# Linear attention and a gated mixture of experts on one core: a list scheduler writes the order, v is copied beside ones, and the first token is routed first

## Chip, cores and metric

One core of one Trainium2 chip runs the whole program. The metric is the device time of one execution in microseconds (us), lower is better. A difference of about 1% is what a measurement of this kernel can tell from no change.

## What is computed

Eight batches (B = 8) of 576 tokens, eight heads of 64 columns. First linear attention for each head, then a mixture of experts whose input x is the attention's output with all heads side by side (512 columns).

```
phi(x) = where(x > 0, x, exp(x) - 1) + 1          # elu + 1
kv = phi(k).T @ v ;  z = sum over s of phi(k)      # 64 x 64 and 64, per head
x  = (phi(q) @ kv) / (phi(q) . z + 1e-6)
logits = x @ w_gate            # 8 experts
local  = sigmoid(x @ w_local)
for s in tokens:
    e = argmax(logits[s]) if s == 0 or local[s] < 0.5 else the expert of token s-1
    p = softmax(logits[s])
    out[s] = p[e] * (relu(x[s] @ w1[e]) @ w2[e])   # w1 512 x 1024, w2 1024 x 512
```

The kernel computes each batch with the expert of its first token and counts on the way the tokens for which another one would be due (`bad`). Only if that count is above 0 does a general path (`general`) run behind it.

## The kernel before

**Tiles.** The eight heads of a batch are two groups `j` of four, so there are 16 pieces `n = 2*a + j` of q, k and v (576 KB each in f32). A piece lies as 128 partitions x 2 x 9 x 64: a partition holds nine consecutive tokens (`c` = 0..8) of a head, 64 partitions a head.

**Attention of a piece.** `exps` (ScalarE, L158) makes exp of k or q; `phi` (VectorE) makes elu + 1 in one of two forms. With `both` ScalarE also does a Relu (L160) and VectorE one operation (L165); without it VectorE does two (L169, L170). `kvs` (TensorE, L179) accumulates the k-v product over the nine `c` in f32, four 64 x 64 tiles of the array at a time. Its moving operand is 128 columns wide: 64 of v and, by a strided view (`vones`), 64 ones that stand once behind each v slot; one column of the sums is z, the other 63 are not read. `kv` is copied out by VectorE (L184). `q_main` and `q_last` transpose q in f32 (L192), ScalarE copies the result out (L203, L212). `num_main` and `num_last` make numerator and denominator (L235, L250, 65 columns), `divide` (VectorE, L218 to L221) divides into bf16 `xb`, `x_part` and `x_last` transpose that (L262, L270) and VectorE copies it into `xT_all` (L264, L271).

**Router.** `logits` (L282, L288) and its copy (L290). The first token of a batch stands in chunk 0, one of the four large chunks, so `pick` (L296 to L310) comes behind the large chunks of a batch. It finds the expert on VectorE, loads the index into a GpSimd register, and GpSimd issues the loads of that expert's w1 and w2 (4 MB in HBM, cast to bf16 on the way). `spread` makes the gate of each token on VectorE.

**Experts.** `hidden(b, m)`, m = 0..7: eight products of 128 x 288 (L364) and a Relu on ScalarE (L367). `output(b, i)`, i = 0..4: L381 for four chunks and L390 for the small one, scaled and copied by ScalarE (L383, L394), which also issues the stores (L386, L396).

**Order.** All engines run in order, in the order in which the program calls these functions, and that is written by hand: batches 0 and 1's attention first, then for each batch `b` the 13 steps (`hidden` 8, `output` 5), and behind each step `s` a piece of the attention of batch b+2 (`after(b, s)`). Each function holds its matrix work and the copy out of PSUM behind it, so an engine's work stands in the order of the steps. The loads of k, q and v go through SyncE's queue; a slot's next load is issued behind the work that frees it (`load_k` in `kvs`, and so on). k and q have three slots each, v four.

## Time and profile before

| | us |
|---|---|
| time, median of 3 runs | 321.84 (320.71 to 323.48) |
| the profiled execution, time | 319.24 |
| its span on the core | 317.5 |
| TensorE busy in the span | 245.4 (77%) |
| VectorE busy | 143.6 (45%) |
| ScalarE busy | 133.2 (42%) |
| GpSimd busy | 16.1 (5%) |
| stretch to the first `hidden` | 67.7 |
| a stage with attention beside the experts (172.02 to 206.46) | 34.44 |
| a stage of the experts alone (275.77 to 293.40) | 17.63 |

A stage here runs from the first `hidden` of a batch to the first `hidden` of the next one. TensorE's clock has two levels, 1.2 and 2.4 GHz; the profile gives the granted clock of a stretch as a share of 2.4 GHz. The profile's busy time of TensorE is that of its matmuls; the weight loads overlap them and are listed apart (PEld). An idle time in brackets behind a row is that of the engine just before the row, with what ended it.

### The profile page before, as it was taken

What the parts mean: (1) busy time and instruction counts of PE and PEld (TensorE: products, weight loads), DVE (VectorE), ACT (ScalarE), POOL (GpSimd) and SP (SyncE); (2) the same over time, 40 slices, a digit from 0 to 9 for tenths busy, and PEclk for the clock granted to TensorE, in tenths of its full rate; (3) what the DMA queues carried; (4) which work ended last, traced back from release to release, by engine and by line L of the source; (5) the groups of instructions that cost most, each with busy time, mean ns of one, the idle gap of its engine ahead of it and who ended that gap; (6) DMA issues with size and microseconds to landing.
All of it is one profiled execution on the core that took longest, in us unless ns stands there. A gap on an engine that the chain in (4) does not pass through costs nothing.

```text
span 317.5 us, 10444 instructions
## 1 busy us (share of the span) xinstructions
PE 245.4 (77%) x4706; PEld 177.0 (56%) x4706; DVE 143.6 (45%) x406; ACT 133.2 (42%) x202; POOL 16.1 (5%) x27
## 2 busy tenths in 40 slices
PE   0635767479779869986998878986798699999891
PEld 0625756357645657464765665564656476675640
DVE  0324373756624565448454762375444844330000
ACT  4545422333137434453346414642455323363541
POOL 1000300001000200001000200020001000020000
PEclk9976578758999999999999999999999979999997
DMA  7991799408980599439973799069513960297304
GB/s 227 391 391 39 198 261 258 152 0 166 257 296 3 163 256 286 163 150 181 267 271 132 147 265 322 4 181 240 85 67 150 166 104 4 97 192 126 151 2 154
DMA packets 29809, 55.27 MB, mean 174 GB/s; under 512 B 2624, under 2 KB 12864, under 8 KB 28736
## 3 DMA queue, kind: packets, MB, share of 16 engines
q0 software_dynamic: 13088, 16.78, 32.0%
q1 hardware_dynamic: 13056, 28.31, 25.1%
q10 hardware_dynamic: 3616, 9.46, 7.9%
q8 instruction: 39, 0.64, 0.8%
q14 instruction: 10, 0.08, 0.1%
HBM read 61.88 MB, written 9.44 MB: 225 GB/s over the span
## 4 chain that ended last, share of the span: by engine, by line
PE 63%; DVE 18%; issue 9%; DMA 3%; ACT 3%; ACTq 2%; SPq 1%; DVEq 0%
PE yps L381 18%; PE hps L364 15%; PE kvps L179 13%; PE nps L235 6%; PE tq L192 4%; DMA qraw<-in_q_dram 3%; PE tx L262 3%; DVE kraw L170 3%; DVE qraw L170 3%; DVE qraw L169 2%; PE yps L390 2%; DVE kraw L169 1%; PE tql L192 1%; PE lps L288 1%; ACTq L386 1%
## 5 line engine op out<-in xcount | busy, mean ns | idle before, releaser
L364 PE MATMUL hps<-xT_all,w1b 128*128 128x288 bf16 x512 | 73.7, 291 | 4.2 <-issue 2.2
L367 ACT ACTIVATE hT<-hps 128x576 bf16<-128x576 f32 x64 | 41.3, 649 | 80.7 <-PE hps L364 74.3
L179 PE MATMUL kvps<-vraw,kraw 64*64 64x128 f32 x1152 | 43.4, 310 | 35.5 <-DVE kraw L170 15.2
L179 PEld LDWEIGHTS kvps<-vraw,kraw 64*64 64x64 f32 x1152 | 39.1, 157 | 40.0 <-DVE kraw L170 17.0
L381 PE MATMUL yps<-w2b,hT 128*128 128x512 bf16 x256 | 59.8, 379 | 0.6 <-issue 0.6
L364 PEld LDWEIGHTS <-w1b 128*128 128x128 bf16 x512 | 46.6, 99 | 19.7 <-issue 7.1
L381 PEld LDWEIGHTS <-hT 128*128 128x128 bf16 x256 | 23.5, 98 | 25.8 <-issue 0.9
L383 ACT ACTIVATE yo<-yps,pr 128x512 f32<-128x512 f32 x32 | 22.0, 688 | 37.4 <-PE yps L381 37.4
L192 PE MATMUL tq<-ident,qraw 64*64 64x64 f32 x1024 | 21.2, 236 | 12.7 <-issue 8.7
L203 ACT COPY qT<-tq 128x512 f32<-128x512 f32 x32 | 18.0, 617 | 30.4 <-PE tq L192 29.7
L192 PEld LDWEIGHTS tq<-ident,qraw 64*64 64x64 f32 x1024 | 18.9, 148 | 16.6 <-issue 12.8
L235 PE MATMUL nps<-kv,qT 64*64 64x65 f32 x1024 | 23.7, 232 | 2.8 <-issue 1.9
L235 PEld LDWEIGHTS nps<-kv,qT 64*64 64x64 f32 x1024 | 19.8, 144 | 8.9 <-issue 7.5
L218 DVE TENSOR_SCALAR den<-nps 128x8 f32<-128x8 f32 x32 | 5.3, 165 | 42.0 <-PE nps L235 41.8
L184 DVE COPY kv<-kvps 128x130 f32<-128x130 f32 x16 | 4.7, 294 | 42.1 <-PE kvps L179 42.1
L221 DVE TENSOR_TENSOR xb<-nps,rec 128x512 bf16<-128x512 f32 x32 | 22.1, 691 | 1.1
L158 ACT ACTIVATE ex<-qraw 128x1152 f32<-128x1152 f32 x16 | 18.5, 1158 | 7.2 <-DVE lt_all L290 6.5
L305 POOL DMA_DIRECT2D w1b<-in_moe_w_dram x9 | 6.9, 766 | 262.7 <-DVE e0f L300 166.0
L158 ACT ACTIVATE ex<-kraw 128x1152 f32<-128x1152 f32 x16 | 18.5, 1156 | 3.6 <-DMA kraw<-in_k_dram 3.6
L264 DVE COPY xT_all<-tx 128x1024 bf16<-128x1024 bf16 (+1 forms) x20 | 11.6, 580 | 11.7 <-PE tx L262 11.7
L170 DVE TENSOR_TENSOR kraw<-kraw,ex 128x1152 f32<-128x1152 f32 x12 | 16.3, 1359 | 0.4
L170 DVE TENSOR_TENSOR qraw<-qraw,ex 128x1152 f32<-128x1152 f32 x12 | 16.3, 1359 | 0.4
(71 smaller groups left out, 178.6 us busy)
## 6 DMA issues: line engine op xcount, KB each, us to landing
kraw<-in_k_dram SPq DMA_DIRECT2D x16, 576.0 KB, 8.5
vraw<-in_v_dram SPq DMA_DIRECT2D x16, 576.0 KB, 10.1
qraw<-in_q_dram SPq DMA_DIRECT2D x16, 576.0 KB, 5.9
out_dram<-yo ACTq DMA_DIRECT2D x16, 512.0 KB, 3.7
w1b<-in_moe_w_dram POOLq DMA_DIRECT2D x7, 1024.0 KB, 10.0
w2b<-in_moe_w_dram POOLq DMA_DIRECT2D x7, 1024.0 KB, 18.3
w1b<-in_moe_w_dram POOLq DMA_DIRECT2D x2, 512.0 KB, 9.0
w2b<-in_moe_w_dram POOLq DMA_DIRECT2D x2, 512.0 KB, 15.1
```

What stands on the lines that cost most here:

```text
L158: nc.scalar.activation(ex_[n, x], raw_, Act.Exp)
L170: nc.vector.tensor_tensor(r, r, e, op=Alu.min)
L179: nc.tensor.matmul(ps[g * PH:(g + 1) * PH, t, :2 * Dh], lhsT=f[t * PH:(t + 1) * PH, g, c, :], rhs=vones(t, s, g, c), start=(c == 0), stop= ...
L192: nc.tensor.matmul(ps[g * PH:(g + 1) * PH, t, at * PH:(at + 1) * PH], lhsT=slot(n, "q")[h, g, c, :], rhs=ident[h, h], start=True, stop=True)
L203: nc.scalar.copy(qT[n][:, t, :SM].rearrange("q (i p r) -> q r i p", i=NC - 1, r=2), ps[:, t, :].rearrange("q (r i p) -> q r i p", i=NC - 1 ...
L221: nc.vector.tensor_tensor(dst, ps[:, :, :, :Dh], rec.rearrange("p g (m o) -> p g m o", o=1).to_broadcast([P, 2, m, Dh]), op=Alu.mult)
L235: nc.tensor.matmul(ps[o * PH:(o + 1) * PH, g, (il * 2 + t) * W:(il * 2 + t + 1) * W], lhsT=qT[n][g * PH:(g + 1) * PH, t, i * P + o * PH:i ...
L264: nc.vector.tensor_copy(xT[a][:, 2 * j:2 * j + 2, i0 * P:i1 * P], ps[:, j, :2 * n].rearrange("p (g s) -> p g s", g=2))
L364: nc.tensor.matmul(ps[:, u, :HS], lhsT=w1b[:, kk, m * P:(m + 1) * P], rhs=xT[b][:, kk, u * HS:(u + 1) * HS], start=(kk == 0), stop=(kk == ...
L367: nc.scalar.activation(hT[b][:, m, :].rearrange("p (u s) -> p u s", u=2), ps[:, :, :HS], Act.Relu)
L381: nc.tensor.matmul(ps[:, 0, :], lhsT=hT[b][:, m, i * P:(i + 1) * P], rhs=w2b[:, m, :], start=(m == 0), stop=(m == FK - 1))
L383: nc.scalar.activation(ym[:, i, :], ps[:, 0, :], Act.Copy, scale=pr[:, i:i + 1])
```

## The change

**Order.** Each function is split into its matrix part and the part that empties PSUM (`kvs` and `kv_out`, and so on). A list of operations with an engine, a length, a rank, needs and a PSUM slot is built in the program, and `in_order` runs a greedy schedule over it; the functions are called in the order that comes out. The stages still lie two batches behind the attention (LEAD = 2) by rank, but the first `hidden` of batch 0 no longer stands behind batch 1's attention.

**v beside ones.** A v piece is copied into `vone` (two buffers, 65 columns for each `c`, the last one all ones), by GpSimd for 15 of 16 pieces and by ScalarE for piece 1. The moving operand of the k-v product is 65 columns wide.

**First token.** The nine token columns are dealt out anew: `c` = 0, with the first token, is the small chunk. q's `c` = 0 of batch 0 is loaded, activated and transposed by itself, first of all. `logits` is done in two parts, the small chunk first, and `pick` follows the small one. w1 and w2 are each issued as one load, also for batch 0, which had two halves.

**phi.** k takes the `both` form in all pieces but piece 0; q as before (`both` in batches 0 and 1 alone). The large chunks' transposes are done for both groups in one PSUM tile with one copy. v has three slots instead of four, the exp buffers are three instead of four.

The core of the diff:

```diff
-        NV = 4
+        NV = 3
+        NE = 3
+        vone = [raw.tile([P, 2, C, W], F32, name=f"vone{i}") for i in range(2)]
...
         def load_q(n):
-            if n < B * NJ:
+            if n < NJ:
+                load(qraw[n % NR][:, :, 1:, :].rearrange("p g c d -> p g (c d)"), q, n, 1, C)
+            elif n < B * NJ:
                 load(qraw[n % NR].rearrange("p g c d -> p g (c d)"), q, n)
+
+        def load_q0(n):
+            load(qraw[n % NR][:, :, 0, :], q, n, 0, 1)
...
+        def v_ones(n):
+            if n == 1:
+                nc.scalar.copy(vone[n % 2][:, :, :, :Dh], vraw[n % NV])
+            else:
+                nc.gpsimd.tensor_copy(vone[n % 2][:, :, :, :Dh], vraw[n % NV])
+
         def kvs(n):
...
-                        nc.tensor.matmul(
-                            ps[g * PH:(g + 1) * PH, t, :2 * Dh],
-                            lhsT=f[t * PH:(t + 1) * PH, g, c, :],
-                            rhs=vones(t, s, g, c), start=(c == 0), stop=(c == C - 1))
+                        nc.tensor.matmul(ps[g * PH:(g + 1) * PH, t, :W], lhsT=f[h, g, c, :],
+                                         rhs=vo[h, g, c, :], start=(c == 0), stop=(c == C - 1))
+
+        def kv_out(n):
             kv[n] = kvp.tile([P, 2, W], F32, name="kv")
-            nc.vector.tensor_copy(kv[n], ps[:, :, :W])
-            load_k(n + NR)
-            load_v(n + NV)
+            nc.vector.tensor_copy(kv[n], open_.pop(("K", n))[:, :, :W])
...
-            nc.vector.max_with_indices(m8, i8, lt_all[0:1, b, 0, :E])
+            nc.vector.max_with_indices(m8, i8, lt_all[0:1, b, NC - 1, :E])
...
+                op(("VC", n), "ACT" if n == 1 else "POOL", 1.16 if n == 1 else 1.8, r - 10, [("lat", "v", n), n >= 2 and ("K", n - 2)],
+                   lambda n=n: v_ones(n))
+                op(("K", n), "PE", 1.25, r, [("P", "k", n), ("VC", n)], lambda n=n: kvs(n), takes="a")
...
+            op(("PK", a), "DVE", 0.45, at - 3, [("RC", a, 0)], lambda a=a: pick(a))
+            for x in range(2):
+                op(("W", a, x), "POOL", 1.0, at + x,
+                   [("PK", a), a >= NW and (("H", a - NW, FK - 1) if x == 0 else ("O", a - NW, NC - 1)),
+                    x and ("W", a, 0)], lambda a=a, x=x: weights(a, x))
...
+                op(("H", a, m), "PE", 1.0, a * NU + m,
+                   [("WL", a, 0), ("XC", a, 0), ("XC", a, 1), ("XLC", a), ("H", a, m - 1) if m else a and ("O", a - 1, NC - 1)],
+                   lambda a=a, m=m: hidden(a, m), takes="m")
...
+        order, begun, done = in_order(ops, {"a": 2, "m": 2, "e": NE}, 0.2)
 
         with tc.manual_schedule():
-
-            for j in range(NJ):
-                exps(j, "k", True)
-                phi(j, "k", True)
-                kvs(j)
...
+            for name in order:
+                run[name]()
```

What `in_order` does at each engine that is free:

```diff
+            for op in queue:
+                name, _, length, rank, needs, takes, gives = op
+                at = now
+                for d in needs:
+                    if d not in done:
+                        break
+                    at = max(at, done[d] + (0.0 if of[d][1] == e else hop))
+                else:
+                    if takes:
+                        if not left[takes]:
+                            continue
+                        at = max(at, left[takes][0])
+                    if at > now:
+                        nxt.append(at)
+                        soon.append((rank, at))
+                    elif best is None or rank < best[3]:
+                        best = op
+            if best and any(r < best[3] - near and t < now + patience * best[2] for r, t in soon):
+                best = None
```

**What stands where now.** TensorE at the start of the program, before (kvps is the k-v product, tq the large q transposes, nps the numerators):

```order
L179 MATMUL kvps<-vraw_77,kraw_71 64x128 x36
L179 MATMUL kvps<-vraw_78,kraw_72 64x128 x36
L192 MATMUL tq<-ident,qraw_74 64x64 x32
L192 MATMUL tq<-ident,qraw_75 64x64 x32
L235 MATMUL nps<-kv,qT 64x65 x32
L262 LDWEIGHTS xb
L262 MATMUL tx<-identb,xb 128x128
```

and of the change (tql and npl belong to the small chunk, lps are its logits):

```order
L252 MATMUL tql<-ident,qraw_74 64x64 x4
L252 MATMUL tql<-ident,qraw_75 64x64 x4
L241 MATMUL kvps<-vone_80,kraw_71 64x65 x36
L241 MATMUL kvps<-vone_81,kraw_72 64x65 x36
L318 MATMUL npl<-kv,qT 64x65 x8
L345 LDWEIGHTS xb_272
L345 MATMUL txl<-identb,xb_272 128x128
...
L252 MATMUL tq<-ident,qraw_74 64x64 x32
L359 LDWEIGHTS xT_all
L359 MATMUL lps<-wg,xT_all 64x9
```

The small chunk's numerators, transposes and logits now stand ahead of the large chunks' numerators; one f32 matmul of this list is two in the profile, so x36 here is x72 there.

VectorE at the boundary of two stages, before (L290 is the copy of the logits, L169 and L170 are phi, L184 the copy of kv):

```order
L290 COPY lt_all<-lps 128x45
L169 TENSOR_SCALAR kraw_71<-kraw_71 128x1152
L170 TENSOR_TENSOR kraw_71<-kraw_71,ex 128x1152
L296 MAX m_2980<-lt_all 1x8
L296 MAX_INDEX i_2981<-m_2980,lt_all 1x8
L300 CAST e0f<-i_2981 1x1
L184 COPY kv<-kvps 128x130
L169 TENSOR_SCALAR qraw_74<-qraw_74 128x1152
L170 TENSOR_TENSOR qraw_74<-qraw_74,ex 128x1152
```

and of the change (L221, L223 and L224 are phi, L338 and L370 the copies of the large chunks' x and logits, L412 the first operation of the gates):

```order
L287 TENSOR_TENSOR xb_2354<-nps,rec_2425 128x512
L221 SCALAR_TENSOR_TENSOR kraw_71<-ex,kraw_71 128x1152
L338 COPY xT_all<-tx 128x4x256 x2
L223 TENSOR_SCALAR qraw_74<-qraw_74 128x1152
L224 TENSOR_TENSOR qraw_74<-qraw_74,ex 128x1152
L370 COPY lt_all<-lps 128x36
L412 TENSOR_REDUCE mx<-lt_all 128x5
```

All four phi of the next stage's pieces (the other two stand some rows further up) are now done ahead of the large chunks' logits, where before phi of k stood behind them and the second k's phi behind the gates.

GpSimd in the middle of the program, before:

```order
L297 TENSOR_LOAD i_1931
L305 ISA
L305 DMA w1b<-in_moe_w_dram 128x4x1024
L310 ISA
L310 DMA w2b<-in_moe_w_dram 128x8x512
```

and of the change (L232 are the copies of v):

```order
L232 COPY vone_80<-vraw_79 128x18x64
L232 COPY vone_81<-vraw_77 128x18x64
L385 TENSOR_LOAD i_1822
L388 ISA
L388 DMA w1b<-in_moe_w_dram 128x4x1024
L392 ISA
L392 DMA w2b<-in_moe_w_dram 128x8x512
```

Two copies now stand between a batch's weight loads and the next one's.

## Rows read from the trace of the kernel before

**Rows 1.** The page: span, and busy time of each engine.

```profile
span 317.5 us, 10444 instructions
PE 245.4 (77%) x4706; PEld 177.0 (56%) x4706; DVE 143.6 (45%) x406; ACT 133.2 (42%) x202; POOL 16.1 (5%) x27
```

**Rows 2.** Busy time by stage: window, us, each engine's busy, granted clock, DMA share, GB/s.

```profile
0.00:67.70 67.70, 35.25 (x951) 31.44 (x952) 28.64 (x82) 29.27 (x35) 4.28 (x13) 0.77 0.75 225
67.70:104.52 36.82, 31.54 (x591) 22.34 (x589) 18.28 (x50) 13.65 (x22) 1.62 (x2) 0.92 0.62 156
...
172.02:206.46 34.44, 28.85 (x591) 20.34 (x589) 18.56 (x50) 15.21 (x24) 1.64 (x2) 1.00 0.75 201
...
275.77:293.40 17.63, 16.97 (x126) 10.89 (x123) 3.70 (x22) 8.45 (x14) 1.63 (x2) 1.00 0.91 187
293.40:317.50 24.10, 15.68 (x110) 9.62 (x108) 0.30 (x2) 8.80 (x14) 0.00 (x0) 0.90 0.26 101
```

**Rows 3.** Timeline, TensorE in the stage from 172.02: start, us, instructions, idle before.

```profile
174.42 2.20 PE L179 MATMUL kvps<-vraw,kraw 64*64 64x128 f32 x72 [1.40 <-issue]
...
179.40 1.16 PE L192 MATMUL tq<-ident,qraw 64*64 64x64 f32 x64 [0.31 <-PE hps L364]
...
184.19 2.20 PE L179 MATMUL kvps<-vraw,kraw 64*64 64x128 f32 x72 [2.54 <-DVE kraw L170]
...
194.91 0.69 PE L235 MATMUL nps<-kv,qT 64*64 64x65 f32 x30 [1.35 <-issue]
```

**Rows 4.** Timeline of the same stage: phi on VectorE, and GpSimd.

```profile
172.18 0.75 DVE L169 TENSOR_SCALAR kraw<-kraw 128x1152 f32<-128x1152 f32 x1
...
176.43 0.89 POOL L310 DMA_DIRECT2D w2b<-in_moe_w_dram  x1
176.88 1.02 DVE L169 TENSOR_SCALAR qraw<-qraw 128x1152 f32<-128x1152 f32 x1
182.77 1.36 DVE L170 TENSOR_TENSOR kraw<-kraw,ex 128x1152 f32<-128x1152 f32 x1
```

**Rows 5.** Chain that ended last, pieces of the same stage: start, us, what.

```profile
187.47 0.63 PE nps L235 x32
...
189.18 1.09 PE tq L192 x64
```

**Rows 6.** Timeline of the start: first loads, products at the lower clock, first pick.

```profile
8.90 1.16 ACT L158 ACTIVATE ex<-kraw 128x1152 f32<-128x1152 f32 x1 [1.26 <-DMA kraw<-in_k_dram]
25.23 1.99 PE L192 MATMUL tq<-ident,qraw 64*64 64x64 f32 x64 [4.89 <-issue]
26.96 1.12 PE L235 MATMUL nps<-kv,qT 64*64 64x65 f32 x32
33.08 0.14 DVE L300 CAST e0f<-i 1x1 f32<-1x1 uint32 x1
34.35 1.63 POOL L305 DMA_DIRECT2D w1b<-in_moe_w_dram  x2 [32.49 <-issue]
```

**Rows 7.** Groups by line and shape: busy, mean ns of one, idle before.

```profile
L165 DVE SCALAR_TENSOR_TENSOR kraw<-ex,kraw 128x1152 f32<-128x1152 f32 x4 | 5.4, 1353 | 6.2 <-ACT kraw L160 6.2
L160 ACT ACTIVATE kraw<-kraw 128x1152 f32<-128x1152 f32 x4 | 4.7, 1163 | 0.1
L221 DVE TENSOR_TENSOR xb<-nps,rec 128x512 bf16<-128x512 f32 x32 | 22.1, 691 | 1.1
L264 DVE COPY xT_all<-tx 128x1024 bf16<-128x1024 bf16 x12 | 8.2, 685 | 8.5 <-PE tx L262 8.5
L126 POOL CAST identb<-ident 128x128 bf16<-128x128 f32 x1 | 0.3, 288 | 0.0
L130 POOL CAST iof<-ioi 128x8 f32<-128x8 int32 x1 | 0.2, 187 | 0.0
```

**Rows 8.** DMA issues: what, queue, count, KB each, median us to landing.

```profile
w1b<-in_moe_w_dram POOLq DMA_DIRECT2D x7, 1024.0 KB, 10.0
w2b<-in_moe_w_dram POOLq DMA_DIRECT2D x7, 1024.0 KB, 18.3
```

More of the change, by code (lines that the diff above doesn't have):

```diff
@@ new lines, in output_out, with op, qslots @@
+                    nc.scalar.dma_start(out=o[:, 0, h * (D // 2):(h + 1) * (D // 2)],
+                                        in_=yl[h * PH:(h + 1) * PH])
+        ops, run = [], {}
+        def op(name, eng, length, rank, needs, fn, takes=None, gives=None):
+            ops.append((name, eng, length, rank, [d for d in needs if d], takes, gives))
+            run[name] = fn
+        NU = FK + NC
+        def qslots(a):
+            old = [n - NQ for n in (a * NJ, a * NJ + 1) if n >= NQ]
+            return [("N", n // NJ, n % NJ, h) for n in old for h in range(2)] +                    [("NL", n // NJ) for n in old]
```

463 lines of the change are left out of this document (247 added, 216 removed).

## The prediction

> **What bounds the kernel now.** I read the page's busy line first, then busy time by stage, then the timeline of one stage, the chain that ended last, and the start. The busy line shows TensorE at 245.4 of 317.5 us and no other engine above half [rows 1], but that is a mean over parts with different limits. By stage [rows 2] there are three:
>
> - the start, 67.70 us in which TensorE has only 35.25 of work, at a mean granted clock of 0.77, and no `hidden` runs;
> - six stages with attention beside the experts, from 67.70 to 275.77, so 34.7 each; the one read closely is 34.44 long with 28.85 of TensorE work at full clock;
> - two stages of experts alone, 17.63 and 24.10 (the last with the final stores), nearly full of work.
>
> So 5.6 us of a middle stage are waits, and the timeline names them [rows 3]: 1.40 and 2.54 ahead of the two k-v products, 0.31 ahead of the q transposes, 1.35 within the numerators; they sum to 5.60. The 2.54 end with phi of k on VectorE (182.77 + 1.36 = 184.13, the product starts at 184.19) [rows 3, 4]. The 1.40 carries the label "issue", but phi of the first k began at 172.18 and takes 0.75 + 1.36 [rows 4], so it ended at 174.3 where the product starts at 174.42 [rows 3]: the same wait. The 1.35 has no releaser; I count it as staying.
>
> **The change, part by part.** All terms are for the profiled execution: 317.5 span, time 319.24, so 1.7 lie outside the span. The median of the runs is 321.84, 2.6 above that execution.
>
> *k-v product, 65 columns for 128.* One piece has 72 matmuls in 2.20, 31 ns each [rows 3]. No 65-column product that accumulates is in the trace. Nearest rows on the same four tiles with as many weight loads: 32 numerators of 65 columns in 0.63, 20 ns each, and 64 transposes of 64 columns in 1.09, 17 ns each [rows 5]. So a piece comes to 1.23 to 1.42 and saves 0.78 to 0.97; I take 0.87, 1.75 per stage. TensorE's work is the largest of a middle stage, so it counts in full: 28.85 - 1.75 = 27.1 of work per stage.
>
> *v copied on GpSimd.* Two copies of 1152 columns per stage. The only copies of that engine in the trace are 128 columns in 288 ns and 8 columns in 187 ns [rows 7]: 0.84 ns for each further column gives 1.15 us, all of 288/128 per column gives 2.6; I take 2. GpSimd has 1.64 of work in 34.44 [rows 2], and a copy can start when the product two pieces back is done, about a stage ahead, so it costs nothing but at the very start. It frees the v slot at the copy instead of at the product, which pays for the fourth slot. Behind the copies on GpSimd's queue stand the weight loads of a batch two stages away, and behind a w2 load, which waits for the last `output` of its buffer, stand copies wanted a stage later: no one is waiting for either.
>
> *phi of k with Relu on ScalarE.* VectorE: 1.35 instead of 0.75 + 1.36 for k [rows 4, 7], 1.5 less per stage, 18.56 to 17.1. ScalarE: two Relu of 1.16 more [rows 7], 15.21 to 17.5; its four store issues, not counted as busy, add some 2.5. Both stay far under 27.1, so nothing from this alone.
>
> *Order.* The order shows phi of both k of a stage ahead of the large logits of the stage before, so the 1.40 and 2.54 go; what is late next is ScalarE at a boundary (last `output` copy, four store issues, then the Relu of the new `hidden`), and there a k-v product and q transposes now stand between the `hidden`s as cover. I keep the 1.35 and allow 0.5 for the rest: 27.1 + 1.9 = 29.0 per stage. Bounds: 27.1 (no wait) and 32.7 (5.6 of waits as now).
>
> *The start.* By the order, the first `hidden` stands behind batch 0's attention and one k-v product, not behind two batches. Worked along its path: the second k was in ScalarE's hands at 8.90, when three large loads had landed [rows 6]; with two small ones ahead the first v is there at about 9.5. Copy 2 (11.5). Two k-v products at the lower clock: 32 numerators took 1.12 there [rows 6], so 72 take 2.5 each (16.5). Then the small chunk to the pick. Before went from its numerators at 26.96 to the pick's end at 33.22 [rows 6], 6.3 for the same kinds of step; the new path is shorter by half its numerators but has 64 transposes of 1.99 in front of the logits [rows 6]: 6 (22.5). From pick to weight issue 33.22 to 34.35, 1.1 [rows 6], and w1 lands 10.0 later [rows 8]: 33.6. Beside that VectorE has, behind the pick, four phi (5.4), four divisions (0.69 and two small operations, about 1.2 each: 4.8) and two copies of 0.7 [rows 7]: 11.6, to 34.1, then a k-v product and logits at the lower clock. First `hidden` at **36**; 33 if phases fall well, 44 if w1 takes the 18.3 that w2's median is [rows 8].
>
> *The first stage* then carries two batches of attention. Experts alone are 16.97 with some small work [rows 2], say 16.4, so attention is 28.85 - 16.4 = 12.4 before and 10.7 now. 16.4 + 2 x 10.7 - 1.4 (the product done early) = 36.4. The stage that now comes first has 31.54 of work against 28.85, 2.7 for the clock that is still low at its beginning (0.92) [rows 2]; with 2 x 1.9 of waits: 43.
>
> *Sum.* 36 + 43 + 5 x 29.0 + 17.63 + 24.10 = 265.7 span, 267.4 with the 1.7 outside, against 319.24. Between that and the same saving off the median (270) I give 268.
>
> **A rule against it.** In the row at 176.88 a one-input operation of VectorE took 1.02 instead of 0.75 while GpSimd was issuing a load [rows 4], so the two hinder one another, and copies of v are far longer users. The Trainium skill (GPSIMD Engine Reference, section 8, Key points) says that GpSimd shares its SBUF interfaces with VectorE and collides with operations in a two-port mode or with two SBUF inputs, and calls VectorE the better place for elementwise work. The row agrees with the first of these. As a mechanism of this kernel: if a copy of length c shuts VectorE out for its whole length, VectorE needs 17.1 + 2c per stage. With c = 2 that is 21.1, under 27.1, and costs nothing; it rules from c = 5.9 (28.9).
>
> **Rivals.**
>
> *Waits come back in the new order (B).* The order was fixed beforehand with lengths; where an engine is late, everything behind it waits. For it: PSUM for attention has two tiles; DMA is busy 0.75 of 34.44 [rows 2], 25.8, which is 89% of a stage of 29.0, so loads may come late. Against: each load is wanted most of a stage after it can be issued. 5 per stage: 36 + 46 + 5 x 32.1 + 41.7 + 1.7 = 286.
>
> *The start does not shorten so far (C).* If routing, copy and weights string out and the first `hidden` begins at 55: 19 more, 287. For it: ScalarE has 13 activations of q and k in a row before its first large q copies are out. Against: before reached its first pick at 33 with a whole large chunk in front.
>
> *GpSimd rules (D), the other side.* The place is VectorE's phi, shut out by copies. The stage at which nothing is gained: 317.5 = 36 + (s + 14) + 5s + 41.7, s = 37.6, so c = 10.3; at c = 11, s = 39.1 and the time is 328. For it: no f32 copy of that length is in the trace. Against: 288 ns for 128 columns is a fifth of the price per column that this needs. Short of it, c = 8 gives 33.1 per stage, about 292.
>
> *No waits at all (E).* 33 + 39 + 5 x 27.1 + 41.7 + 1.7 = 251.
>
> **How the numbers follow.** My forecast, own range 256 to 280: 0.62. B 0.17, C 0.08, D 0.06 (half of it short of the break-even point, half within 1% or slower), E 0.07. Leaving out D, the lower half of E and the upper third of B and C (0.18 together) gives 252 to 289. Only D's half ends at no gain (0.01 within 1%) or slower by over 1% (0.02; with 0.01 for what I have not thought of 0.03), so faster by over 1% is 0.96; 1% is about what a measurement of this kernel can tell.
>
> **What would show it.** Right: first `hidden` near 36; 72 k-v matmuls in 1.2 to 1.4; middle stages of 29 with at most 2 of idle TensorE; no k-v product that waits for phi. GpSimd copies near 2 with VectorE's phi at most a few tenths longer. Wrong: TensorE idle ahead of the numerators or `hidden` for ScalarE's copies (B), w1 landing after 40 or the pick after 30 (C), copies above 6 or phi far above 1.36 (D).

## The result and the profile after

| | before | after |
|---|---|---|
| time, median of 4 runs each, same chip | 322.66 us (320.71 to 324.56) | 280.22 us (278.88 to 282.19) |
| ratio, 95% interval | | 0.869 (0.861 to 0.877) |
| the profiled execution: time, span | 319.24, 317.5 | 279.97, 278.2 |
| stretch to the first `hidden` | 67.6 | 35.9 |
| the first stage | 36.8 | 43.5 |
| the next five stages together | 171.4 | 156.1 |
| the two stages of experts alone | 41.7 | 42.75 |

The kernel is 13% faster, and of the 39.3 us that the profiled span lost, 25.0 lie in the start and the first stage together, 15.3 in the next five stages; 1.0 is given back at the end. The kernel before is cut here at its first `hidden` itself, 67.56; the 67.70 of the earlier table lies 0.14 behind it. Here and below, medians are over all executions of a kernel, while ratios leave out its slower ones, so where the two disagree the ratio decides. The page of the changed kernel, which answers to [rows 1]:

```profile
span 278.2 us, 10449 instructions
PE 225.1 (81%) x4689; PEld 161.5 (58%) x4706; DVE 140.3 (50%) x396; ACT 146.8 (53%) x218; POOL 35.1 (13%) x42
...
q8 instruction: 39, 0.64, 0.9%
```

TensorE works 20.3 us less and idles 19.0 less. Busy time by stage, cut at the first `hidden` of each batch (as [rows 2]: window, us, busy of PE, PEld, DVE, ACT, POOL, granted clock, DMA share, GB/s):

```profile
0.00:35.87 35.87, 19.27 (x549) 16.97 (x550) 21.22 (x40) 25.97 (x31) 8.99 (x17) 0.76 0.97 300
35.87:79.38 43.51, 35.47 (x896) 25.73 (x897) 29.82 (x84) 23.60 (x36) 6.02 (x6) 0.92 0.90 247
79.38:115.64 36.26, 30.34 (x689) 22.45 (x688) 24.08 (x66) 20.83 (x30) 5.42 (x6) 0.95 0.89 222
115.64:146.05 30.41, 26.43 (x593) 18.86 (x591) 19.26 (x53) 16.94 (x26) 3.94 (x4) 1.00 0.90 224
146.05:177.34 31.29, 28.15 (x587) 19.50 (x589) 17.88 (x50) 17.39 (x26) 3.93 (x4) 0.95 0.82 202
177.34:206.98 29.64, 26.51 (x587) 18.85 (x588) 14.43 (x47) 13.91 (x23) 4.30 (x4) 1.00 0.69 153
206.98:235.45 28.47, 26.60 (x588) 18.91 (x589) 10.81 (x43) 10.78 (x20) 1.64 (x2) 1.00 0.61 118
```

From 35.87 to 235.45, 199.58 us, TensorE has 173.5 of work and 26.1 of idle time. The timeline of TensorE shows what is idle there (start, us, instructions, idle before; two stretches of the stage from 115.64, as [rows 3]):

```profile
117.69 1.28 PE L241 MATMUL kvps<-vone,kraw 64*64 64x65 f32 x72
...
123.83 1.16 PE L241 MATMUL kvps<-vone,kraw 64*64 64x65 f32 x63
126.72 0.35 PE L241 MATMUL kvps<-vone,kraw 64*64 64x65 f32 x9 [1.73 <-issue]
126.89 0.65 PE L299 MATMUL nps<-kv,qT 64*64 64x65 f32 x32
...
130.04 1.04 PE L252 MATMUL tq<-ident,qraw 64*64 64x64 f32 x55
132.88 0.38 PE L252 MATMUL tq<-ident,qraw 64*64 64x64 f32 x9 [1.81 <-issue]
```

From the first `hidden` on, no k-v product waits for phi in front of it any more, as [rows 3] had it twice per stage. Instead a product stops in its middle, nine matmuls before its end, and TensorE stays idle though the profile shows no engine that it waits for. Such an idle time is called a hole below. There are eleven between 35.87 and 235.45, from 1.14 to 3.59 us, 22.3 us together, and all the rest of the idle time is 3.8. The DMA view holds what they have in common. The queue named instruction moves packets of 0.64 MB / 39 = 16 KB; two of its rows (number of packets, MB, share of 16 engines), the first from the window 124.4 to 124.5, the second from 130.45 to 130.5:

```profile
q8 instruction: 1, 0.02, 57.6%
q8 instruction: 1, 0.02, 122.1%
```

57.6% of 16 engines in 0.1 us is 0.92 us of one engine, 122.1% in 0.05 us is 0.98. So one packet ends at 125.4 and TensorE goes on at 126.72, the other at 131.45 and it goes on at 132.88. All eleven holes end 1.2 to 1.5 us after the end of such a packet. Counted in TensorE's records (weight loads and matmuls), they stand on one grid: 126.72 and 132.88 are 257 apart, and every distance from one hole to the next is 1, 3, 4 or 5 times 256, within 3. The packets that end a hole take 0.9 to 1.1 us, no longer than others (0.9 to 1.5), so what is late is their start. The theory that follows, FETCH: TensorE had used up the instructions that it had, and the next ones came late.

Where four of the holes end (at 46.24, 69.62, 101.31 and 155.10; they are 1.82 to 3.59 long) the granted clock is also low: 0.50, the level of 1.2 GHz, from 46.1 to 49.5, 70.1 to 73.4, 100.9 to 104.1 and 155.5 to 158.7. Everywhere else between 35.87 and 235.45 it is at the upper level. So a hole seems to cost more than its idle time; that it is the reason for the lower clock was not tested by itself.

The start (as [rows 6]), first copy of v, pick, weight issue and first `hidden`, and three groups (as [rows 5, 7]: busy, mean ns of one, idle before):

```profile
9.57 1.31 POOL L232 COPY vone<-vraw 128x1152 f32<-128x1152 f32 x1 [7.62 <-DMA vraw<-in_v_dram]
...
20.63 0.14 DVE L378 CAST e0f<-i 1x1 f32<-1x1 uint32 x1
...
21.91 0.89 POOL L388 DMA_DIRECT2D w1b<-in_moe_w_dram  x1 [2.90 <-issue]
...
35.87 1.14 PE L453 MATMUL hps<-xT_all,w1b 128*128 128x288 bf16 x8
```

```profile
L241 PE MATMUL kvps<-vone,kraw 64*64 64x65 f32 x1152 | 24.0, 239 | 10.2 <-DVE wg L607 5.5 <-issue 4.7
...
L232 POOL COPY vone<-vraw 128x1152 f32<-128x1152 f32 x15 | 19.6, 1304 | 84.2 <-PE kvps L241 55.6 <-issue 15.0 <-DMA vraw<-in_v_dram 13.6
...
L221 DVE SCALAR_TENSOR_TENSOR kraw<-ex,kraw 128x1152 f32<-128x1152 f32 x15 | 20.2, 1350 | 3.3 <-ACT kraw L212 3.3
```

### The profile page after: what moved, and what is told of

It reads as the page before. It is cut to its first block, busy times and chain, and to the rows that moved or that the text cites. A ratio compares the mean times of both kernels' runs of the same rounds, so it can differ in the third digit from the quotient of the medians.

```text
span 278.2 us, 10449 instructions
## 1 busy us (share of the span) xinstructions
PE 225.1 (81%) x4689; PEld 161.5 (58%) x4706; DVE 140.3 (50%) x396; ACT 146.8 (53%) x218; POOL 35.1 (13%) x42
## 4 chain that ended last, share of the span: by engine, by line
PE 76%; issue 11%; DVE 4%; ACT 3%; ACTq 2%; DMA 2%; SPq 0%; DVEq 0%
PE hps L453 23%; PE yps L470 20%; PE kvps L241 8%; PE tq L252 7%; PE nps L299 6%; PE tx L333 3%; PE yps L474 2%; DMA kraw<-in_k_dram 2%; PE npl L318 1%; PE lps L365 1%; ACTq L488 1%; ACTq L493 1%; PE eb L400 1%; ACT ex L210 1%; PE tql L252 1%
## 5 line engine op out<-in xcount | busy, mean ns | idle before, releaser
L470 PE MATMUL yps<-w2b,hT 128*128 128x512 bf16 x239 | 58.5, 385 | 1.8 <-issue 1.0
L453 PEld LDWEIGHTS <-w1b 128*128 128x128 bf16 x512 | 47.8, 100 | 19.9 <-issue 6.2
L241 PE MATMUL kvps<-vone,kraw 64*64 64x65 f32 x1152 | 24.0, 239 | 10.2 <-DVE wg L607 5.5
L241 PEld LDWEIGHTS kvps<-vone,kraw 64*64 64x64 f32 x1152 | 21.4, 151 | 16.0 <-issue 10.3
L232 POOL COPY vone<-vraw 128x1152 f32<-128x1152 f32 x15 | 19.6, 1304 | 84.2 <-PE kvps L241 55.6
L252 PE MATMUL tq<-ident,qraw 64*64 64x64 f32 x1024 | 22.1, 235 | 7.6 <-issue 5.3
L299 PEld LDWEIGHTS nps<-kv,qT 64*64 64x64 f32 x1024 | 20.3, 149 | 10.6 <-issue 9.2
L210 ACT ACTIVATE ex<-qraw 128x1152 f32<-128x1152 f32 (+2 forms) x18 | 18.9, 1052 | 6.0 <-DMA qraw<-in_q_dram 3.9
L221 DVE SCALAR_TENSOR_TENSOR kraw<-ex,kraw 128x1152 f32<-128x1152 f32 x15 | 20.2, 1350 | 3.3 <-ACT kraw L212 3.3
L212 ACT ACTIVATE kraw<-kraw 128x1152 f32<-128x1152 f32 x15 | 17.5, 1164 | 0.5
L224 DVE TENSOR_TENSOR qraw<-qraw,ex 128x1152 f32<-128x1152 f32 x12 | 16.3, 1359 | 0.4
```

The costliest lines, as they stand in the source:

```text
L210: nc.scalar.activation(ex_[n, x][:, :, c0:c1, :], raw_, Act.Exp)
L221: nc.vector.scalar_tensor_tensor(r, e, 1.0, r, Alu.min, Alu.add)
L232: nc.gpsimd.tensor_copy(vone[n % 2][:, :, :, :Dh], vraw[n % NV])
L241: nc.tensor.matmul(ps[g * PH:(g + 1) * PH, t, :W], lhsT=f[h, g, c, :], rhs=vo[h, g, c, :], start=(c == 0), stop=(c == C - 1))
L252: nc.tensor.matmul(ps[g * PH:(g + 1) * PH, t, at * PH:(at + 1) * PH], lhsT=slot(n, "q")[h, g, c, :], rhs=ident[h, h], start=True, stop=True)
L299: nc.tensor.matmul(ps[o * PH:(o + 1) * PH, g, (il * 2 + t) * W:(il * 2 + t + 1) * W], lhsT=qT[n][g * PH:(g + 1) * PH, t, i * P + o * PH:i ...
```

## The experiments

Three theories compete to explain the holes: FETCH (instructions come late behind the loads), DENSITY (they come late, but however full the DMA queues are), OTHER (waits for other engines). Times are medians, ratios are against the kernel before on the same chip; 280.2 and 0.869 are the change's own. The landings in the first expectation are read against a zero that was 0.39 us off: the 0.8 to 1.1 us named there are 1.2 to 1.5.

### Few weight loads

```diff
         def weights(b, x):
-            if x == 0:
+            if b >= NW:
+                wt[b] = wt[b - NW]
+            elif x == 0:
```

> Theories for the idle time that TensorE of the changed kernel has inside its attention work (11 holes of 1.1 to 3.6 us, 22.3 us in all, each without a releaser, each ending 0.8 to 1.1 us after a 16 KB packet of the DMA queue named instruction has landed, and 256 instructions of TensorE apart). FETCH: TensorE runs out of instructions, because 256 of the 64 x 64 f32 products are used up in 2.2 us and their successors come late behind the bulk loads. DENSITY: the same, but a fetch takes as long as it does whether or not the DMA queues are full. OTHER: the holes are waits for other engines or for PSUM in the new order, and the packets are a coincidence. This kernel loads w1 and w2 for batches 0 and 1 only; batches 2 to 7 use these weights again, so their output is left wrong in part (the loads' queue held 37.9% of the 16 DMA engines' time). FETCH: holes 22.3 down to under 8, time 280 down to 264 to 270. DENSITY and OTHER: holes stay at 18 or more, time 276 to 282.

Measured: 264.1 us, ratio 0.821 (0.813 to 0.828). Busy time of its fourth to sixth stage, in which the DMA share has fallen from 0.61 to 0.82 down to 0.47 and less:

```profile
141.42:168.06 26.64, 25.96 (x588) 18.66 (x589) 17.60 (x50) 17.14 (x26) 2.30 (x2) 1.00 0.47 158
168.06:194.26 26.20, 25.88 (x588) 18.52 (x589) 14.28 (x47) 13.98 (x23) 2.30 (x2) 1.00 0.27 93
194.26:220.86 26.60, 26.19 (x587) 18.72 (x589) 10.52 (x43) 10.84 (x20) 0.00 (x0) 1.00 0.13 47
```

The same products in the same order, and TensorE idles at most 0.7 us in a stage. Five holes are left, 10.5 us, all before 129; the packets that end them begin at 36.28, 43.17, 68.35, 97.06 and 126.02. The page's row of the DMA share, 40 slices of 6.58 us each:

```profile
DMA  6999999559985096058804840460040003004003
```

All five packets lie in slices of 0.8 or more (the 6th, 7th, 11th, 15th and 20th). The five holes stand before the same instructions of TensorE as five of the eleven, those that end at 39.33, 46.24, 69.62, 101.31 and 132.88 in the change. OTHER falls, for nothing that TensorE's products need in these stages changed but w1 and w2, for which it did not wait, and waits for other engines have no reason to stand on a grid of 256 instructions; DENSITY falls, for the stream of instructions is the same. The 10.5 are above the 8 that FETCH expected, the time is as it expected.

### Products of 128 columns, with and without the weight loads

```diff
-                        nc.tensor.matmul(ps[g * PH:(g + 1) * PH, t, :W], lhsT=f[h, g, c, :],
-                                         rhs=vo[h, g, c, :], start=(c == 0), stop=(c == C - 1))
+                        o = (g * C + c) * W
+                        nc.tensor.matmul(ps[g * PH:(g + 1) * PH, t, :2 * Dh], lhsT=f[h, g, c, :],
+                                         rhs=vo[h, o:o + 2 * Dh], start=(c == 0), stop=(c == C - 1))
```

> One part undone: the moving operand of the k-v product is 128 columns wide again (65 of v and ones, then what lies behind them; the extra sums are not read). One piece then takes 2.20 where it takes 1.21 now, 16 x 0.99 = 15.8 us more TensorE work. By the prediction's term for this part the whole of it shows: 280 + 15.8 = 296. OTHER says the same, 293 to 299. FETCH and DENSITY: the 144 instructions of a product are used up at half the rate, and a part of the holes goes: 285 to 291.

Measured: 281.0 us, ratio 0.873 (0.861 to 0.885): no difference from the change, less than any theory expected. Page and group of this kernel:

```profile
PE 234.2 (84%) x4689; PEld 172.2 (62%) x4706; DVE 140.4 (50%) x396; ACT 146.8 (53%) x218; POOL 34.6 (12%) x44
...
L244 PE MATMUL kvps<-vone,kraw 64*64 64x128 f32 x1152 | 39.9, 290 | 7.5 <-POOL vone L234 5.4
```

The products cost 39.9 - 24.0 = 15.9 us more, as they should. Of this 9.2 come out of the idle time (278.2 - 225.1 = 53.1 in the change, 278.1 - 234.2 = 43.9 here; the holes over 0.45 us shrink from 22.3 to 10.6), and 6.8 because TensorE's other work got shorter; the mean granted clock of this execution is 0.969 where the change has 0.939, and of the four stretches at 0.50 behind holes one is left, from 155.3. So with all loads running, the 65 columns are worth nothing: what they save, TensorE loses again, in part to waiting for instructions and in part to the lower clock. The second run takes the loads away as well:

> Two of the earlier edits together: the moving operand of the k-v product 128 columns wide, and w1 and w2 loaded for batches 0 and 1 only (so that the output of batches 2 to 7 is partly wrong). With all weight loads the wide operand cost nothing (281.0 against 280.2), with the loads taken away and 65 columns the time was 264.1. FETCH: where the loads do not delay the instructions, the wide operand costs most of its 15.8 us: 274 to 280. If the width never matters, because something else than TensorE and its instructions sets the stage: 262 to 267. DENSITY (a fetch takes as long with few loads as with many) gives no difference between the two pairs: 264 to 266.

Measured: 268.6 us, ratio 0.846 (0.841 to 0.851), against 264.1 and 0.821 with 65 columns; 4.5 us by the medians, 8 by the ratios (the two ran on different chips). Its stages that answer to the three above:

```profile
140.36:168.40 28.04, 27.72 (x587) 20.25 (x589) 17.78 (x50) 17.27 (x26) 2.31 (x2) 1.00 0.45 150
168.40:196.44 28.04, 27.72 (x587) 20.25 (x588) 14.46 (x47) 14.11 (x23) 2.30 (x2) 1.00 0.25 87
196.44:224.49 28.05, 27.73 (x588) 20.26 (x589) 10.63 (x43) 10.84 (x20) 0.00 (x0) 1.00 0.12 45
```

Where no instruction is late, the width shows: 28.04 against 26.64, 26.20 and 26.60, 1.56 us per stage, close to the prediction's 1.75. The expected 274 to 280 was too high, because this holds only in the stages with few loads; in the first ones the holes (3.6 us here, 10.5 with 65 columns) still make up for it. The time also lies just above the 262 to 267 of "the width never matters", so it is the stages, and not the time, that decide between the two.

### Products cut in two

```diff
-                op(("K", n), "PE", 1.25, r, [("P", "k", n), ("VC", n)], lambda n=n: kvs(n), takes="a")
+                op(("K1", n), "PE", 0.7, r, [("P", "k", n), ("VC", n)], lambda n=n: kvs(n, 0, 5), takes="a")
+                op(("KG", n), f"kg{n}", GAP, 0, [("K1", n)], lambda: None)
+                op(("K", n), "PE", 0.55, r, [("KG", n)], lambda n=n: kvs(n, 5, C))
```

The transposes of q (Q) are cut in the same manner, GAP is 0.6.

> The order alone: each k-v product and each transposition of q is cut into two halves, and the scheduler is told to leave 0.6 us between the halves, so that it puts a block of hidden (16 instructions in 1.05 us) there. Instructions, loads and engines' work are the same. FETCH and DENSITY: a run of f32 products is now at most 144 instructions where it was 272 or more, so the holes fall from 22.3 to under 10 us and the time from 280 to 264 to 271. OTHER: the same work waits for the same engines, 277 to 284; longer if the PSUM tile, held longer, is what is waited for.

Measured: 276.9 us, ratio 0.856 (0.843 to 0.869). Neither number is what FETCH expected (holes under 10, 264 to 271): the holes shrink from 22.3 to 14.8 us only, and the time by 3 us, within the uncertainty and at the edge of OTHER's 277 to 284. The order of this kernel shows why: the first half of a k-v product now often stands directly before the first half of a q transposition, so the runs are half as long, not gone, and in other places new waits came (1.29 us for w1 at the first `hidden`). So it does not separate the theories as it was meant to: its time settles nothing, and the smaller holes agree with FETCH.

### Half the instructions

```diff
-        vone = [raw.tile([P, 2, C, W], F32, name=f"vone{i}") for i in range(2)]
+        vone = [raw.tile([P, 2, C, W], BF16, name=f"vone{i}") for i in range(2)]
...
+            if True:
+                if (n, x) not in qb:
+                    qb[n, x] = qbp.tile([P, 2, C, Dh], BF16, name=x + "b")
...
-                nc.vector.scalar_tensor_tensor(r, e, 1.0, r, Alu.min, Alu.add)
+                nc.vector.scalar_tensor_tensor(d, e, 1.0, r, Alu.min, Alu.add)
...
-            kv[n] = kvp.tile([P, 2, W], F32, name="kv")
+            kv[n] = kvp.tile([P, 2, W], BF16, name="kv")
...
-                                     lhsT=slot(n, "q")[h, g, c, :], rhs=ident[h, h],
+                                     lhsT=qb[n, "q"][h, g, c, :], rhs=identb[h, h],
...
-                qT[a * NJ + j] = qtp.tile([P, 2, S], F32, name="qT")
+                qT[a * NJ + j] = qtp.tile([P, 2, S], BF16, name="qT")
```

> Half the instructions for the same products: phi of q and of k, the copy of v, the transposed q and kv are kept in bf16 instead of f32, so that each product of the attention is one pass of load and matmul instead of two (3,456 of TensorE's 9,412 instructions fall away). Loads and the experts are as in the changed kernel. FETCH: the holes of 22 us go almost wholly, and the attention's 80 us of TensorE work halve; a stage is then set by the DMA queues (busy 76% of 278 us, 212 in all) or by the experts' own 16.4 with 5 of attention: 235 to 250. OTHER: the work falls by 40 us, but the waits of 22 us stay: 238 to 262. A time above 265 would say that TensorE and its instructions are not what sets a stage at all.

Measured: 243.3 us, ratio 0.764 (0.755 to 0.773): it beats both kernels, at the price of bf16 operands in the attention. From its page, and three of its stages:

```profile
PE 184.5 (76%) x2962; PEld 120.5 (50%) x2978; DVE 140.3 (58%) x396; ACT 146.0 (60%) x218; POOL 34.7 (14%) x42
...
q8 instruction: 25, 0.41, 0.7%
...
DMA kraw<-in_k_dram 21%; PE yps L479 16%; PE hps L462 11%; DMA qraw<-in_q_dram 7%; ACT ex L211 5%; ACTq L502 4%; ACT kraw L213 3%; ACTq L497 3%; ACT hT L469 3%; ACT yo L494 3%; ACT qT L274 3%; PE tx L342 2%; SPq L144 1%; PE nps L308 1%; ACT yl L500 1%
```

```profile
73.88:102.11 28.23, 24.24 (x440) 16.16 (x439) 24.07 (x65) 20.22 (x30) 5.42 (x6) 0.99 1.04 271
102.11:126.29 24.18, 21.50 (x377) 14.14 (x375) 19.15 (x53) 16.89 (x26) 4.09 (x4) 1.00 1.04 277
126.29:153.22 26.93, 23.26 (x372) 15.04 (x373) 17.38 (x50) 17.18 (x26) 3.94 (x4) 0.94 0.97 255
```

There are 25 packets of instructions instead of 39, and from the first `hidden` on not one hole without a releaser over 0.45 us, though the DMA share is 0.97 to 1.04 in the stages shown. The time alone would fit OTHER too (238 to 262); the holes decide. TensorE's work falls by 40.6 us, the span by 35.6. The next bound is in view: the chain that ended last has 28% in the loads of k and q, and the DMA engines are busy all of these stages.

### An order written by hand

```diff
-        order, begun, done = in_order(ops, {"a": 2, "m": 2, "e": NE}, 0.2)
+        order = by_hand()
```

`by_hand` calls the same functions in an order after that of the kernel before, each PSUM tile emptied right behind its products.

> The order alone undone: all other parts of the change stay (65 columns, copies of v, first token in the small chunk, phi of k), but the functions are called in an order written by hand after that of the kernel before: batches 0 and 1's attention ahead of the first hidden, then one piece of attention behind each step. By the prediction's terms: first hidden at 60 to 65 instead of 36, a middle stage of 27.1 of work and 4 to 5 of waits, 31.5; 62 + 6 x 31.5 + 41.7 + 1.7 = 294, range 288 to 300. If the order is worth nothing beside the other parts: 280. FETCH adds: the holes that end with an instruction packet are fewer than in the changed kernel's order (under 15 us), since one piece of attention at a time stands between two blocks of the experts.

Measured: 326.2 us, ratio 1.016 (1.007 to 1.026): all other parts of the change together, without the scheduler's order, are no gain. The first `hidden` stands at 69.67 and the stages are 33 to 37 long. VectorE and TensorE in the stage from 140:

```profile
149.12 1.35 DVE L221 SCALAR_TENSOR_TENSOR kraw<-ex,kraw 128x1152 f32<-128x1152 f32 x1
...
150.57 1.64 PE L241 MATMUL kvps<-vone,kraw 64*64 64x65 f32 x72 [3.72 <-issue]
```

The second k-v product waits 3.72 for phi of k, which ends at 150.47 and stands on VectorE behind the gates: the wait of [rows 3], longer. Holes over 0.45 us that end with an instruction packet are 7.3 us in all, fewer than in the change, as FETCH has it. The 294 was too low: the expectation gave a middle stage 4 to 5 us of waits (the six have 5.3 to 7.9) and a start of 62. It also gave the stage 27.1 of TensorE work, where these stages have 28.0 to 30.5 in spite of the narrower products: their granted clock is 0.86 to 0.95, where the kernel before has 1.00 in four of its six. It is one order of many and not tuned, so it bounds what the other parts are worth in an order like the old one, not what the best hand-written one would give.

### 65 columns alone, in the kernel before

```diff
-                            lhsT=f[t * PH:(t + 1) * PH, g, c, :],
-                            rhs=vones(t, s, g, c), start=(c == 0), stop=(c == C - 1))
+                            lhsT=f[t * PH:(t + 1) * PH, g, c, :],
+                            rhs=vo[t * PH:(t + 1) * PH, g, c, :], start=(c == 0), stop=(c == C - 1))
...
-            load_v(n + NV)
+            copy_v(n + 2)
```

`copy_v` is GpSimd's copy into `vone`, followed by that slot's next load.

> One part of the change alone, in the kernel before: v is copied beside ones by GpSimd (three v slots, two 65-column buffers, a copy called behind the k-v product two pieces back) and the k-v product is 65 columns wide. Order, phi, first token as before. By the prediction's term, 0.99 us less TensorE work for each of 16 pieces, in full: 322 - 15.8 = 306 (302 to 310). In the order of before the product waits for phi of k, and what follows it is TensorE's own work, so the term should hold. FETCH: four to six holes of 1.5 to 2 us that end with an instruction packet come in addition: 308 to 315. No gain (318 or more): then the width paid nothing in the old order either.

Measured: 316.9 us, ratio 0.988 (0.976 to 1.001): by the ratio some 4 us of the expected 15.8, and no gain at all is inside the interval. The holes of FETCH are few here; the loss is elsewhere. VectorE, GpSimd and TensorE in the stage from 172:

```profile
173.96 0.89 DVE L174 TENSOR_SCALAR qraw<-qraw 128x1152 f32<-128x1152 f32 x1
174.89 2.82 DVE L175 TENSOR_TENSOR qraw<-qraw,ex 128x1152 f32<-128x1152 f32 x1
175.33 1.16 POOL L108 COPY vone<-vraw 128x1152 f32<-128x1152 f32 x1
...
177.81 1.16 PE L196 MATMUL tq<-ident,qraw 64*64 64x64 f32 x64 [1.64 <-issue]
...
182.65 1.28 PE L183 MATMUL kvps<-vone,kraw 64*64 64x65 f32 x72 [2.58 <-issue]
```

phi's second operation takes 2.82 beside a copy of 1.16, where it takes 1.36 alone [rows 4]: 1.46 more. That is the copy's 1.16 and 0.30 besides, and GpSimd is still issuing the load of w2 when the operation begins. Its first operation takes 1.64 to 2.10 beside a copy in other stages, 0.75 alone. The q transposes, which waited 0.31 [rows 3], wait 1.64 for it, and the second product still waits 2.58. The whole stage, to be read against the one of 34.44 in [rows 2]:

```profile
169.72:203.88 34.16, 28.38 (x595) 19.53 (x591) 20.79 (x50) 15.24 (x24) 4.09 (x4) 0.95 0.70 185
```

Its idle time is 5.78 as against 5.60 (1.56 ahead of the first product, then these two), so nothing is gained there: VectorE, with 20.79 of work for 18.56, sets the products' starts. TensorE's work is 28.38 for 28.85, although two products take 1.84 less, because the granted clock is 0.95 for 1.00 and the other products got longer. The clock is 0.50 from 184.0 to 187.2, right behind the second product and its wait of 2.58, and likewise in the two stages before (115.7 to 118.9, 149.8 to 153.0); in the kernel before, the product of 128 columns at 184.19, with its wait of 2.54, was followed by no such stretch. So the narrower products gain nothing here for two reasons, the unchanged waits and the lower clock; why the clock fell here and not there stays open.

### The pick behind the large chunks

```diff
-                       [("E", x, n), c0 and ("P0", n), c0 and (("PK", 0) if n else ("DL", 0)),
-                        0 < a < LEAD and ("PK", 0)],
+                       [("E", x, n), c0 and ("P0", n), c0 and ("DL", 0),
+                        0 < a < LEAD and ("DL", 0)],
...
-            op(("PK", a), "DVE", 0.45, at - 3, [("RC", a, 0)], lambda a=a: pick(a))
+            op(("PK", a), "DVE", 0.45, at - 3, [("RC", a, 0), ("RC", a, 1)], lambda a=a: pick(a))
```

Some phi of the first two batches were ranked behind the pick; with a later pick they follow the small chunk's division (`DL`) instead.

> One part undone: the pick of a batch waits for the logits of its large chunks too (as in the kernel before, where the first token stood in a large chunk); the small chunk is still computed first. w1 of batch 0 is then issued behind the large logits, some 12 us later than at 21.9, and the scheduler, which knows it, puts batch 1's attention ahead of the first hidden: first hidden at 44 to 48 instead of 36.0, the stage behind it shorter by what was done ahead. By the prediction's terms, work that TensorE does in the gap is not lost: 281 to 286. If the first token's place is what makes the start short, all of the delay shows: 289 to 293.

Measured: 286.0 us, ratio 0.891 (0.881 to 0.901); the four executions took 282.3, 283.4, 288.6 and 289.4, and the first is the profiled one (span 280.2). w1 of batch 0 is issued at 32.86 and the first `hidden` begins at 45.36, with 1.76 of it waiting for w1:

```profile
32.86 0.89 POOL L388 DMA_DIRECT2D w1b<-in_moe_w_dram  x1 [1.06 <-DVE ex L414]
45.36 0.90 PE L453 MATMUL hps<-xT_all,w1b 128*128 128x288 bf16 x3 [1.76 <-DMA w1b<-in_moe_w_dram]
```

The first stage is 35.41 instead of 43.51, so of 9.5 us of delay 8.1 come back, as the first theory had it. What is left is small and not well measured: 2.0 us by the two profiled spans, 7 by the ratios, which come from different chips. Of the 31.7 us by which `hidden` starts earlier, all but these 9.5 are there without the early pick.

### Copies twice, and phi of k in two operations

```diff
-                nc.gpsimd.tensor_copy(vone[n % 2][:, :, :, :Dh], vraw[n % NV])
+                for _ in range(2):
+                    nc.gpsimd.tensor_copy(vone[n % 2][:, :, :, :Dh], vraw[n % NV])
```

> The disputed cost doubled: GpSimd makes each copy of v twice, 1.15 us more for 15 pieces. If the copies are hidden, as the prediction has it, only those of the start show: 280 to 283. If a copy shuts VectorE out for its whole length (rival D), VectorE has 2.3 more per stage, 21 to 24 of 30, and what waits for it comes later: phi of k or q beside a copy goes from 1.36 to over 2.3, and the time to 283 to 290.

Measured: 284.2 us, ratio 0.892 (0.883 to 0.902): 4 us by the medians, one more than expected and inside the 283 to 290 that rival D was given, so the time does not decide. In the profiled execution (281.4 us, span 279.6, the shortest of its four) the first `hidden` is 2.2 later, and from there to the end of the sixth stage it is 199.5 long against 199.6: the cost is at the start. VectorE is shut out there (a phi of 2.23 at 26.91 beside two copies), and in the stages only beside small operations. The change itself shows why its copies hurt so little, at 127:

```profile
127.22 1.15 POOL L232 COPY vone<-vraw 128x1152 f32<-128x1152 f32 x1 [6.95 <-PE kvps L241]
128.04 0.69 DVE L287 TENSOR_TENSOR xb<-nps,rec 128x512 bf16<-128x512 f32 x1
```

A copy beside VectorE's division, whose large input is in PSUM, leaves it at 0.69 [rows 7]; the two overlap by 0.33 here, and in the run with two copies a division at 71.2 lies wholly beside them and takes 0.69 too. At 90.25 a gate operation with both inputs in SBUF took 1.07 instead of 0.19 beside a copy. The order lays the copies there, not beside phi. At the start, where a copy and phi do meet, the copy gets longer, and so does the second phi beside it:

```profile
23.66 1.35 DVE L221 SCALAR_TENSOR_TENSOR kraw<-ex,kraw 128x1152 f32<-128x1152 f32 x1
23.68 2.33 POOL L232 COPY vone<-vraw 128x1152 f32<-128x1152 f32 x1
24.99 2.23 DVE L221 SCALAR_TENSOR_TENSOR qraw<-ex,qraw 128x1152 f32<-128x1152 f32 x1
```

The other part undone by itself, phi of k:

```diff
-    BOTH = "k"
+    BOTH = ""
```

> One part of the change undone: phi of k by two operations of VectorE in batches 2 to 7 (0.75 + 1.36 instead of 1.35), without the Relu on ScalarE; the scheduler knows the lengths. VectorE has 1.5 more per stage, ScalarE 2.3 less. By the prediction, nothing from this alone: 277 to 283. If ScalarE's waits at the boundary of the stages (its k loads, the stores it issues, the Relu) are what keeps TensorE, it gets faster: 272 to 276.

Measured: 280.9 us (277.0 to 286.3): no difference within this spread, as expected; its holes are 22.7 us.

### Two attempts beyond the bf16 version

The same edit of BOTH in the bf16 version:

> The version with bf16 operands in the attention (243.3) has no instruction hole left; its TensorE waits for ScalarE (hidden for the Relu of the one before 9.9 us, numerators for the copy of q 8.2, output for the scaled copy 4.3). Here phi of k is two operations of VectorE, without ScalarE's Relu: ScalarE 17.5 us less, VectorE 11 more. If ScalarE is what now ends the stages: 236 to 241. If VectorE or the DMA queues are: 243 to 248.

Measured: 247.2 us, ratio 0.772 (0.763 to 0.781). The time is in the range of "VectorE or the DMA queues": without ScalarE's Relu, and with more work on VectorE in its place, nothing is gained. Which of the two ends the stages stays open.

```diff
-                        nc.scalar.dma_start(out=o[:, 1 + (NC - 1) * r:NC + (NC - 1) * r, :],
+                        nc.sync.dma_start(out=o[:, 1 + (NC - 1) * r:NC + (NC - 1) * r, :],
```

(and the small chunk's store the same.)

> The version with bf16 operands in the attention, with the stores issued by SyncE instead of ScalarE: ScalarE has four issues of 0.6 us per stage less, 19 us in all, at the stage's boundary where hidden waits for it. If ScalarE is what now ends the stages: 236 to 241. If a store at the head of SyncE's queue delays the loads behind it more than that: 244 to 252.

Measured: 257.7 us, ratio 0.801 (0.793 to 0.810), slower than expected at worst. The waits of SyncE's queue in the profiled execution, the longest of its five with 260.5 (for what, us in total, times, longest):

```profile
SPq L497 <- ACT yo L494: 134.3, 8, 25.8
```

A store at the head of the queue waits for its chunks up to 25.8 us, and the loads of k stand behind it; exp of k then waits 25.3 us for them in all, where the bf16 version waits 11.0.

## Why the prediction was right, and where it was off

The sign was right, and 280.2 lies in the wide range of 252 to 289; it is 12 us from the centre of 268 and just outside the forecast's own range of 256 to 280. The middle stages, forecast at 29.0 with at most 2 of idle TensorE, came to 31.2 on average with 1.9 to 5.9 idle, nearer to rival B's 32.1. By its steps:

- **First `hidden` at 36**: 35.87. Copy, pick (20.77 against 22.5) and weight issue (21.91 against 23.6) were each a little early, VectorE's work behind them filled the rest.
- **First stage 43**: 43.51, but by two errors that cancel: 35.5 of work and 8.0 of waits, where I had 39.2 and 3.8. Some of the second batch's attention went into the next stage (30.34 of work for 27.1).
- **A k-v product of 1.23 to 1.42**: 1.28 for 72 matmuls at full clock (the row at 117.69), inside the range: 0.92 saved for the 0.87 taken. The 1.21 that an expectation above names for it is too low by the same row.
- **TensorE's work**: 27.1 in each of five stages and 39.2 in the first, 174.7; measured 173.5.
- **A copy of 2 us, 1.15 to 2.6**: 1.15 where nothing is beside it, 2.33 beside two phi at 23.68. That it costs nothing but at the start holds, but only in this order: beside the old one's phi it doubles VectorE's operations.
- **phi of k**: 1.35, nothing from it alone, as the run with two operations shows.
- **The failed step: "I keep the 1.35 and allow 0.5 for the rest".** Waits were put at 1.9 for a stage, and twice that for the first stage, which carries two batches: 7 x 1.9 = 13.3 in all; they are 26.1. "The rest" was right: 26.1 - 22.3 = 3.8, 0.54 for each. The 1.35 "within the numerators" was taken as a constant, because it had no releaser. It has the marks of a wait for instructions: it ends at 194.91 [rows 3], 1.3 after a packet that ends at 193.65 (116.8% of 16 engines in 0.05 us is 0.93 us, from the DMA view of the kernel before for the window 192.70 to 192.75):

```profile
q8 instruction: 1, 0.02, 116.8%
```

   Over its six stages the kernel before has four such holes over 0.45, 5.8 us in all; the change, which packs the same instructions into less time, has 22.3. Per batch of attention that is 3.2 (22.3 / 7) where 1.35 was kept. The 12.8 of it and 1.0 in the last two stages, less 1.2 of work and 0.1 of the start, are the 12.5 by which the span of 278.2 is above the 265.7.
- **Rival B** had the right shape (waits come back in the new order, about 5 per stage, 286) for the wrong reason: 22.3 of the 26.1 are not waits for loaded data or for PSUM, but for TensorE's own instructions. **Rival C** did not come: the pick ends at 20.77 and the first `hidden` begins at 35.87. **Rival D's** mechanism is real, as the 2.82 beside a copy of 1.16 shows; its place was wrong, since the order lays the copies elsewhere, and at 1.15 it is far from its break-even of 10.3. The rule of the Trainium skill (GPSIMD Engine Reference, section 8, Key points) that the prediction weighed, that GpSimd collides with operations of VectorE with two SBUF inputs, agrees with the 2.82. That the division, with an input in PSUM, stays at 0.69 is shown by this case's rows alone. **Rival E** (no waits) is what the stages with few loads come to: 26.2 to 26.6.

So the gain is, as far as these runs show, that of the order: it removed the waits of [rows 3] and brought the first `hidden` forward. Of the other parts, the 65 columns, the early pick and phi of k were each undone alone, which cost nothing that can be told from no change for two of them and 2 to 7 us for the pick; all parts together in the one order written by hand gain nothing; the scheduler's order without the other parts was not run. The 65 columns, the part that the prediction priced most carefully, are worth 1.6 us a stage where instructions arrive in time and the clock is at its upper level, and nothing measurable in the change as it is. That fewer loads take the holes away is shown by a run that changes nothing else on TensorE; with bf16 operands they go as well, but there TensorE also has 40.6 us less work and waits more for ScalarE. What stays open is why a fetch starts so late behind loads: when it is asked for, no view tells.

## What to carry to other kernels

An idle time of TensorE in the middle of a run of small f32 products, without a releaser, is to be looked up among the packets of the instruction queue before it is taken for a constant: here it grew when the stages got shorter, and the granted clock was low behind four of the eleven. Where it was there, a product with half the columns paid nothing; fewer instructions for the same products (one pass instead of two), or fewer loads at that moment, took it away. A copy moved to GpSimd cost nothing beside the division that reads PSUM, and held up, or was held up by, operations with their inputs in SBUF, so where it is called decides its price. A narrower product gained nothing in the order that left its waits as they were.

## What was not expected of the hardware

- TensorE can run out of instructions: 11 holes, 22.3 us of a span of 278.2, each ending 1.2 to 1.5 us after a packet of 16 KB, beside a DMA share of 0.61 to 0.90. With the share at 0.47 and below and the same instructions there are none. The Trainium skill (Runtime: NRT & Kernel Launch, Instruction fetch mechanics) describes the 16 KiB blocks of 256 instructions, fetched ahead by a DMA queue, and calls the cost of crossing a block "mostly hidden". The blocks agree with the trace; the cost does not where f32 products of 64 x 64 use up a block while bulk loads run, and here the measurement decides.
- A GpSimd copy of 1152 f32 columns took 1.15 us by itself. Beside VectorE operations with two SBUF inputs one or both got longer: at 174.89 of the run with 65 columns alone the operation took 2.82 instead of 1.36 and the copy 1.16; at 23.68 of the change the copy took 2.33, the first phi beside it its usual 1.35, and the second 2.23.
